# A planned three-stage kernel: new prices for VectorE's turns and GpSimd's copies, and one causal row block turned by way of DRAM

## The chip, the core and the metric

The kernel runs as one program on one core of a Trainium2 chip. The metric is the device time of one execution in microseconds (us); less is better. The core has five engines with a queue of instructions each: TensorE (PE; its weight loads are PEld), VectorE (DVE), ScalarE (ACT), GpSimd (POOL) and SyncE (SP), which here only issues DMAs. An engine takes its queue in order: an instruction that waits holds up all behind it.

## The reference

Three stages follow each other. All tensors are float32, except where a factor in the setup makes one float64 (the kernel decodes those on the chip).

```python
# 1. attention, masked by hash buckets: B, H, S, D = 2, 8, 768, 64; proj is 64 x 6
q_bits = (einsum('bhsd,dk->bhsk', q, proj) > 0); k_bits = the same of k
mask = bucket(q_bits)[:, :, :, None] == bucket(k_bits)[:, :, None, :]
scores = where(mask, q @ k^T / 8, -1e9);  attn = softmax(scores);  x = attn @ v       # as B, S, 512
# 2. four causal attention experts (512 -> 64), the best two of each token, weighted
for e in range(4):
    qe, ke, ve = x @ wq[e], x @ wk[e], x @ wv[e]
    a = softmax(where(causal, -1e9, qe @ ke^T / 8));  ye = a @ ve @ wo[e]
    out += gate[e] * ye
# 3. mixing of tokens and of channels on x = out: 2 x 768 x 512
theta = x @ w_theta;  zr, zi = x * cos(theta), x * sin(theta)
u = x + einsum('ts,bsd->btd', w_tok_r, zr) + einsum('ts,bsd->btd', w_tok_i, zi)
result = u + relu(u @ w_ch)
```

## The kernel before

**The work.** Stage 1 goes over 8 pairs of heads (2 batches of 4 pairs), stage 2 over the two expert pairs of both batches, stage 3 over blocks of 128 tokens. In stages 1 and 2 the unit of work is a `Unit`, a block of 128 query rows against up to 768 keys. For each: `scores` (TensorE, into a PSUM tile `ps`), `low` (VectorE: scale and row maximum, from `ps` to the tile `T`, L1007), `exp` (ScalarE, in place in `T`, L1015), `flip` (the turn of the row block, so that keys lie on partitions) and, for a whole group of units, `mix` (TensorE: the product with the values, L1060 in stage 1, L1082 in stage 2), and `gather` (ScalarE and GpSimd bring the product into `ob`).

**Two ways to turn.** In stage 1 eleven of a head pair's twelve row blocks are turned by VectorE in 32x32 pieces (L1022, 88 in all); their `mix` is 96 small matmuls on 32 rows (L1060), 192 records in the trace. All other blocks, and all of stage 2's, are turned by TensorE: one transpose for 128 columns into PSUM (L1026) and a copy back to `T` by ScalarE (L1035). Stage 3 has a third way in use already, for blocks of `u`: VectorE turns 32x32 pieces (`uw`, L1686), a DMA writes them to DRAM (`u_d`, L1688), and four DMAs bring them back with the pieces in their places (`uv`, L1690), before ScalarE reads them (L1698).

**Copies between partitions.** `shift` (L742) moves half a tile to other partitions by the engine that a letter names: A is ScalarE, P is GpSimd (`hi_pool`, L739), D is a DMA on SP's queue. `MOVESU` gives the letters of the four moves of `unstash`, which fetches an expert's operands back from DRAM (tile `op`) in stage 2.

**What sets the order.** The order of each engine's queue is not the order of the code. `Plan` reads the finished program, and `price` gives each instruction a step (when the engine is free for the next) and a latency, in ns. `forward` places the instructions one after the other, on the engine that can start first, with ranks from `backward`; `NUDGES` are random shifts of the ranks in a stretch of time; `fix` then writes the order into the program. The prices are used at build time alone. The lists `LP`, `PREP`, `LATE`, `FUSE`, `FM` and the like say beside which unit a job is written, which sets the order of tiles in the pools. `SPARE` is the number of extra matmuls on zeros (L867) in the first waits of TensorE. In `forward` the constants `FETCH` stand for TensorE's own instructions being fetched in parts of 256.

Of the kernel before, what the change touches and what calls it, by code (L numbers as in the profile page):

```python
# [38 lines left out]
LP = [0, 4.5, 5.5, 2.5, 8.5, 6, 9, 13, 10, 15.0, 17.5, 15]  # L39
PREP = [13.5, 9, 7.0, 9, 7.5]  # L40
# [6 lines left out]
LATE = [0, 2, 1, 1, 1, 1, 3, 4, 4, 4]  # L47
# [12 lines left out]
FUSE = 62  # L60
FS = 5
FM = 5
# [17 lines left out]
STAY = [[1, 4], [0, 5]]  # L80
MERGE = [11, 12]
MOVEG = 'P'
MOVESB = 'PD'
MOVESU = 'AADP'
# [3 lines left out]
LINE2 = [[[(0, 4)], [(0, 5)]], [[(1, 4)], [(1, 5)]], [[(0, 2), (1, 2)], [(0, 3), (1, 3)]],  # L88
# [6 lines left out]
SPARE = 35  # L95
# [100 lines left out]
def price(o):  # L196
# [20 lines left out]
    if o.eng == "DVE":  # L217
        if "Transpose" in o.kind and n > 32:
            return 215 + n * 1.045, 250 + n * 1.045
        crosses = o.r and o.r[0][2][0] // 32 != o.w[0][2][0] // 32  # L220
        if n < 30:
            s = 240 if o.kind == "InstReciprocal" else 170
        elif o.kind == "InstTensorScalarPtr" and src == ["S"]:
            s = 66 + n / 1.92
        else:
            s = 75 + n * 1.036
        if crosses:
            s = max(s, 80 + n * 1.18)
        if len(o.w) > 1:
            return 82 + n * 1.045, 202 + n * 1.045  # L230
        elif len(o.r) > 2 and o.kind == "InstTensorScalarPtr":
            s = 270 + n * 1.05
        return s, s + 80
# [10 lines left out]
    s = 140 + n * 2.17 if o.kind == "InstTensorTensor" else 165 + n * 0.82  # L244
# [463 lines left out]
def fused(ctx: ExitStack, tc: tile.TileContext, qT, kT, vP, vN, projd, wqk_d, wvg, wo, woT, wth, wtok, wch, out, waits, turns, runs,  # L708
          orders, desk, families, sequence):
    nc = tc.nc  # L710
# [95 lines left out]
    v_d = dram.tile([128, NT * E * D], F32, name="v_d")  # L806
    u_d = dram.tile([B * NT, 128, DM], F32, name="u_d")
# [16 lines left out]
    def ps_tile():  # L824
        return ps.tile([128, 1024], F32, name="ps", tag="ps", bufs=3)
# [125 lines left out]
    class Unit:  # L951


        def __init__(self, grp, rows, rs, last=False):
            self.grp, self.rs = grp, rs
            self.parts, off = [], 0
            for side, i in rows:
                w = (i + 1) * 128 if grp.causal else S
                self.parts.append((side, i, off, w))
                off += w  # L960
            self.w = off
            grp.done |= {(side, i) for side, i in rows}
            self.band = not grp.causal and rows[0][1] < NT - rs.old
            if not grp.causal:
                self.ends = rows[0][0] if last else None
                return
            ends = [c for c in range(NT // 2) if c not in grp.ended
                    and {(s, 2 * c + a) for s in (0, 1) for a in (0, 1)} <= grp.done]
            self.ends = ends[0] if ends else None
            grp.ended |= set(ends)  # L970
# [22 lines left out]
        def low(self):  # L993
# [3 lines left out]
            if not self.grp.causal:  # L997
                rs.n = self.parts[0][1] * NT
            self.P = rs.T[:, rs.n:rs.n + nb, :]
            for side, i, off, w in self.parts:  # L1000
                self.grp.at[side, i] = rs.T, rs.n + off // 128
# [18 lines left out]
        def flip(self):  # L1020
            if self.band:
                nc.vector.transpose(self.ss, self.ss)  # L1022
                return
            self.pt = ps_tile()
# [3 lines left out]
        def copy(self):  # L1028
            if self.band:
                return  # L1030
# [6 lines left out]
        def mix(self):  # L1037
# [36 lines left out]
            for j in range(n1):  # L1074
                for side in (0, 1):
                    (PT, a0), (_, a1) = g.at[side, 2 * c], g.at[side, 2 * c + 1]
                    half = slice(side * 64, side * 64 + 64)
                    if j < n0:
# [768 lines left out]
```

## Time and profile before

| | us |
|---|---|
| three runs, median (lowest, highest) | 496.0 (494.62, 496.75) |
| the profiled execution | 493.23 |
| its span, first to last instruction | 491.4 |
| TensorE busy | 465.1 (95%) |
| VectorE busy | 386.3 (79%) |
| ScalarE busy | 329.6 (67%) |
| GpSimd busy | 288.5 (59%) |

The profiled execution took 1.8 us more than its span, and 0.56% less than the median of the three runs. In its trace stage 1 of the first batch lies at about 9 to 125 us, stage 2's projections of the first batch and stage 1 of the second at 115 to 230, stage 2's units at 205 to 327, stage 3 from 305 to the end. A row of the views by instruction has start, duration, engine, line, operation, out<-in, and in brackets how long the engine was idle before and what ended that. "issue" as releaser means that the profile shows nothing that was waited for.

### The profile page before, as it was taken

To read this page: it belongs to the slowest core of one execution; us is meant where nothing else is said; L and a number is where in the kernel's file an instruction comes from. 1 tells how busy PE (TensorE), PEld (TensorE's weight loads), DVE (VectorE), ACT (ScalarE), POOL (GpSimd) and SP (SyncE) were. 2 spreads that over 40 slices of the span, in tenths; PEclk is the share of its full clock that TensorE was granted. 3 is DMA by queue.
4 is the path that set the end of the run, shared out by engine and by line. 5 is a ranking of instruction groups with operands and counts; after the bars stand their busy time and mean duration, and the time that the engine had idled before them with its cause. 6 is when DMAs were issued, how large, how long until landed. Compare 5 with 4: busy or idle time off the path is not lost.

```text
span 491.4 us, 13377 instructions
## 1 busy us (share of the span) xinstructions
PE 465.1 (95%) x5360; PEld 374.0 (76%) x5360; DVE 386.3 (79%) x668; ACT 329.6 (67%) x658; POOL 288.5 (59%) x243
## 2 busy tenths in 40 slices
PE   8889988989999999898999999999999999999997
PEld 3576866677898777676789877778888888878886
DVE  6999999688894999896677684849869999676543
ACT  7788867586454978869767689997667666571110
POOL 6997999888248479226920046058557697874000
PEclk9999999899999999999999999999999999999999
DMA  7544535445785545873448324512443445470542
GB/s 245 175 140 135 162 120 157 116 149 166 195 301 174 173 151 155 232 254 108 134 150 238 99 75 134 187 38 55 145 144 131 148 151 151 109 209 34 168 145 85
DMA packets 44249, 74.17 MB, mean 151 GB/s; under 512 B 6948, under 2 KB 13892, under 8 KB 44188
## 3 DMA queue, kind: packets, MB, share of 16 engines
q1 hardware_dynamic: 42028, 69.80, 46.4%
q10 hardware_dynamic: 2160, 3.52, 1.9%
q8 instruction: 42, 0.69, 0.6%
q14 instruction: 19, 0.16, 0.1%
HBM read 54.52 MB, written 15.91 MB: 143 GB/s over the span
## 4 chain that ended last, share of the span: by engine, by line
PE 72%; DVE 10%; ACT 7%; issue 4%; POOL 3%; DMA 2%; DVEq 0%; POOLq 0%; ACTq 0%
PE ps L1671 19%; PE ps L986 9%; PE ps L1060 9%; PE ps L1381 6%; PE wk L1585 5%; DVE T L1007 5%; PE wk L1600 4%; PE O L1060 4%; PE ps L1318 4%; PE ps L1026 4%; PE O L1082 3%; PE ps L1600 3%; ACT T L1015 3%; DVE T L1022 3%; PE ps L1068 1%
## 5 line engine op out<-in xcount | busy, mean ns | idle before, releaser
L1015 ACT ACTIVATE T<-T,m 128x768 f32<-128x768 f32 (+3 forms) x144 | 121.2, 844 | 31.8 <-DVE T L1007 31.2
L1007 DVE TENSOR_SCALAR_CACHE_REDUCE T<-ps 128x768 f32<-128x768 f32 (+3 forms) x144 | 115.5, 834 | 32.2 <-PE ps L991 15.0
L1022 DVE STREAM_TRANSPOSE T<-T 128x768 f32<-128x768 f32 x88 | 82.5, 960 | 5.5 <-ACT T L1015 5.1
L1671 PE MATMUL ps<-zh,tok 128*128 128x512 f32 x240 | 76.7, 390 | 0.0
L1060 PE MATMUL ps<-T,V 32*64 32x160 f32 (+1 forms) x1536 | 63.9, 312 | 8.4 <-DVE T L1007 3.3
L1060 PE MATMUL O<-T,V 32*64 32x160 f32 (+1 forms) x1536 | 65.0, 312 | 4.8 <-issue 4.7
L1060 PEld LDWEIGHTS ps<-T,V 32*64 32x64 f32 x1536 | 54.7, 131 | 13.9 <-issue 5.2
L986 PE MATMUL ps<-op 128*128 128x512 f32 (+5 forms) x256 | 60.1, 343 | 1.1 <-DVE op L1211 0.9
L1060 PEld LDWEIGHTS O<-T,V 32*64 32x64 f32 x1536 | 50.1, 131 | 6.4 <-issue 6.3
L1671 PEld LDWEIGHTS ps<-zh,tok 128*128 128x128 f32 x240 | 45.1, 188 | 9.7
L1671 PE MATMUL ps<-zl,tok 128*128 128x512 f32 x120 | 46.3, 391 | 0.0
L802 POOL TENSOR_TENSOR tok<-raw,tok 128x512 fp32r<-128x512 f32 x27 | 41.6, 1550 | 7.9 <-PE ps L1671 4.3
L986 PEld LDWEIGHTS ps<-op 128*128 128x128 f32 (+1 forms) x256 | 39.3, 191 | 8.4 <-issue 2.7
L1035 ACT COPY T<-ps 128x768 f32<-128x768 f32 (+2 forms) x36 | 28.6, 798 | 9.0 <-PE ps L1026 8.5
L739 POOL TENSOR_SCALAR op<-op 64x768 fp32r<-64x768 f32 x8 | 6.8, 853 | 45.6 <-ACT op L1397 28.7
L1026 PE MATMUL ps<-ident,T 128*128 128x128 f32 x216 | 30.7, 277 | 1.8 <-ACT T L1015 1.1
L1107 POOL TENSOR_TENSOR ob<-ob,W 64x768 f32<-64x768 f32 x16 | 29.4, 1835 | 1.3
L1026 PEld LDWEIGHTS ps<-ident,T 128*128 128x128 f32 x216 | 23.7, 141 | 5.8 <-ACT T L1015 2.5
L1015 ACT ACTIVATION_READ_ACCUMULATOR T<-T,m 128x1 f32 x144 | 27.2, 189 | 0.0
L1671 PEld LDWEIGHTS ps<-zl,tok 128*128 128x128 f32 x120 | 22.5, 188 | 4.9
L986 PE MATMUL ps<-op,sql 128*128 128x512 f32 x84 | 24.2, 366 | 2.1 <-DVE T L1007 1.1
L1620 POOL TENSOR_TENSOR kk<-kk,x 128x512 f32<-128x512 f32 x12 | 17.8, 1482 | 13.3 <-ACT kk L1619 13.3
(236 smaller groups left out, 1161.6 us busy)
## 6 DMA issues: line engine op xcount, KB each, us to landing
V<-in_vP_dram SPq DMA_DIRECT2D x48, 256.0 KB
raw<-in_wtok_dram SPq DMA_DIRECT2D x36, 256.0 KB
raw<-tok_d SPq DMA_DIRECT2D x27, 256.0 KB
tok_d<-g SPq DMA_DIRECT2D x18, 256.0 KB
rT<-r_d SPq DMA_DIRECT2D x22, 192.0 KB
qk_d<-op SPq DMA_DIRECT2D x8, 384.0 KB
op<-qk_d SPq DMA_DIRECT2D x8, 384.0 KB
out_dram<-o ACTq DMA_DIRECT2D x11, 256.0 KB
```

The source lines that it names most:

```text
L802: nc.gpsimd.tensor_sub(l, raw, f(h))
L986: one = nc.tensor.matmul(self.sp[:, c0:c1], lhs, rhs[:, c0 - off:c1 - off], start=a == 0, stop=last)
L1007: i = nc.vector.tensor_scalar(self.ss[:, off:off + w], self.sp[:, off:off + w], -0.125, NEG, op0=OP.mult, op1=OP.min, accum_out=m)
L1015: e = nc.scalar.activation(self.ss[:, off:off + w], self.ss[:, off:off + w], AF.Exp, bias=m, scale=-1.0, accum_out=self.grp.den[:, side, i ...
L1022: nc.vector.transpose(self.ss, self.ss)
L1026: nc.tensor.transpose(self.pt[:, j * 128:(j + 1) * 128], self.P[:, j, :], ident)
L1035: nc.scalar.copy(self.P, src)
L1060: together(nc.tensor.matmul(o[a][half * 64:half * 64 + 64, 0:nb * 32], V[band, n // 4, (n - a) % 4], T[band, 0:nb, n * 32:n * 32 + 32], st ...
L1107: nc.gpsimd.tensor_add(g.ob[keep], g.ob[keep], W[keep])
L1381: nc.tensor.matmul(pp[:, c0:c1], lhs[:, kd, e, :], rhs[kd][:, c0:c1], start=n == 0, stop=n == 3 * NK - 1)
L1600: nc.tensor.matmul(o, lhs[:, sl], rhs[:, kd, cols], start=n == 0, stop=n == 3 * NK - 1)
L1671: nc.tensor.matmul(yp[t], lhs[:, a, t, :], rhs[:, a], start=i == 0 and a == 0 and n == 0, stop=i == NT - 1 and a == 1 and n == 2)
```

## The change

Four things change in the code.

1. **Prices.** A turn by VectorE goes from 215 + 1.045 n ns to 95 + 1.045 n (n columns), its three-operand form from 270 + 1.05 n to 110 + 1.05 n; a copy by GpSimd from 165 + 0.82 n to 165 + 0.96 n, its two-operand form above 600 columns from 2.17 n to 2.28 n. With them the lists of places and all `NUDGES` are new (48 before, 78 now), so that the queues' orders differ nearly everywhere.
2. **One row block goes by DRAM.** Row block 5 (768 keys) of the first head of the second batch's first expert pair is turned like a block of `u`: one turn by VectorE into a tile `far`, one DMA to `far_d`, four back into `T`. Its six transposes on TensorE and its copy on ScalarE go. Its `mix` reads the block with other strides, so that the two row blocks that shared a matmul of 256 columns get one of 128 each: 67 instead of 72 with 256, 34 instead of 24 with 128.
3. **The last of `unstash`'s four moves** goes from GpSimd to a DMA (4 of them).
4. In stage 2 row block 5 comes ahead of row block 4, in places of `T` that are fixed for both; one extra matmul on zeros more.

```diff
-LP = [0, 4.5, 5.5, 2.5, 8.5, 6, 9, 13, 10, 15.0, 17.5, 15]
-PREP = [13.5, 9, 7.0, 9, 7.5]
+LP = [2, 4.5, 5.5, 2.5, 8.5, 6, 9, 13, 10, 15.0, 17.5, 15]
+PREP = [13.5, 9, 5.0, 9, 7.5]
-LATE = [0, 2, 1, 1, 1, 1, 3, 4, 4, 4]
+LATE = [0, 2, 1, 2, 1, 1, 3, 4, 4, 4]
-FUSE = 62
+FUSE = 60
-FM = 5
+FM = 3
+FAR = [4]
-MOVESU = 'AADP'
+MOVESU = 'AADD'
-LINE2 = [[[(0, 4)], [(0, 5)]], [[(1, 4)], [(1, 5)]], [[(0, 2), (1, 2)], [(0, 3), (1, 3)]],
+LINE2 = [[[(0, 5)], [(0, 4)]], [[(1, 4)], [(1, 5)]], [[(0, 2), (1, 2)], [(0, 3), (1, 3)]],
-SPARE = 35
+SPARE = 36
-    (288489, 5.7, 61.8, -1706), (998291, 190.5, 209.2, -4780), (727432, 453.6, 518.1, -1623), (283489, 92.7, 185.6, -838),
+    (403328, 264.5, 297.2, 538), (801660, 280.3, 290.3, 3416), (839062, 460, 492.5, -4580), (434552, 329.2, 405.9, -2079),
...
         if "Transpose" in o.kind and n > 32:
-            return 215 + n * 1.045, 250 + n * 1.045
+            return 95 + n * 1.045, 230 + n * 1.045
...
         elif len(o.r) > 2 and o.kind == "InstTensorScalarPtr":
-            s = 270 + n * 1.05
+            s = 110 + n * 1.05
...
-    s = 140 + n * 2.17 if o.kind == "InstTensorTensor" else 165 + n * 0.82
+    s = 140 + n * (2.28 if n > 600 else 2.17) if o.kind == "InstTensorTensor" else 165 + n * 0.96
...
+            self.far = grp.causal and rows[0][1] == 5 and 2 * grp.number - 8 + rows[0][0] in FAR
...
+            elif self.parts[0][1] > 3:
+                rs.n = self.parts[0][0] * 11 + (self.parts[0][1] - 4) * 5
...
+            if self.far:
+                w = pool.tile([128, S], F32, name="far", tag="far", bufs=1)[:, :self.w]
+                nb = self.w // 128
+                nc.vector.transpose(w.rearrange("p (b j x) -> p b j x", b=4, x=32),
+                                    self.ss.rearrange("p (j b x) -> p b j x", b=4, x=32))
+                d = far_d[next(fars)][:, :self.w]
+                nc.sync.dma_start(d, w)
+                for m in range(4):
+                    nc.sync.dma_start(self.ss[32 * m:32 * m + 32].rearrange("i (n y) -> i n y", n=4),
+                                      d.rearrange("(n i) (m y) -> m i n y", n=4, m=4)[m])
+                return
...
+                    one = g.at[side, 2 * c + 1][0]
+                    if isinstance(one, Unit):
+                        if j < n0:
+                            together(nc.tensor.matmul(self.O[half, 0], g.V[:, j, side, :], PT[:, a0 + j, :], start=j == 0,
+                                                      stop=False), j == side == 0, self.rs)
+                        rhs = one.ss.rearrange("p (n j x) -> p j n x", n=4, x=32)[:, j]
+                        together(nc.tensor.matmul(self.O[half, 1], g.V[:, j, side, :], rhs, start=False, stop=j == n1 - 1),
+                                 False, self.rs)
+                        continue
```

**SP's queue, the third head pair** (about 73 to 86 us of the trace before). `wraw`: expert weights, `V`: values, `raw<-in_kT`: keys, `r_d` and `rT`: softmax factors, out to DRAM and back. Before:

```order
L910 DMA r_d<-rows 4x32x32
L847 DMA wraw<-in_wqk_dram 128x512
L1151 DMA V<-in_vP_dram 128x512
L1134 DMA raw<-in_kT_dram 128x768
L1151 DMA V<-in_vP_dram 128x512 x2
L913 DMA rT<-r_d 64x768 x2
L847 DMA wraw<-in_wvg_dram 128x260
```

And now, the same place:

```order
L857 DMA wraw<-in_wvg_dram 128x260
L1184 DMA V<-in_vP_dram 128x512 x3
L1167 DMA raw<-in_kT_dram 128x768
L920 DMA r_d<-rows 4x32x32
L1184 DMA V<-in_vP_dram 128x512
L923 DMA rT<-r_d 64x768 x2
L1184 DMA V<-in_vP_dram 128x512 x2
```

The big weights `in_wqk` have left this group, and `r_d`, which waits for VectorE, now stands in the middle of it, ahead of `rT`.

**TensorE, between the fifth and the sixth `mix` of stage 1** (L1060 before, L1084 now; in the trace before the sixth starts at 80.11 us). Before, 20 score matmuls stand there, of which these are the last ones:

```order
L986 MATMUL ps<-skl,sqh 128x512
L986 MATMUL ps<-skl,sqh 128x256
L986 MATMUL ps<-skh,op 128x512
L986 MATMUL ps<-skh,op 128x256
L986 MATMUL ps<-skl,sqh 128x512
L986 MATMUL ps<-skl,sqh 128x256
L1060 MATMUL ps<-T,V 64x160 x4
L1060 MATMUL O<-T,V 64x160 x4
```

Now there are 24 and six transposes; this is the middle:

```order
L997 MATMUL ps<-skh,op 128x512
L997 MATMUL ps<-skh,op 128x256
L997 MATMUL ps<-skl,sqh 128x512
L997 MATMUL ps<-skl,sqh 128x256
L1050 MATMUL ps<-ident,T 128x128 x6
L997 MATMUL ps<-skh,op 128x512
```

Four score matmuls and a turn by TensorE have come between the two.

**VectorE and TensorE at the row block that goes by DRAM** (second batch's first expert pair). Before, on VectorE, the `low` of the pair's blocks (L1007) follow each other, with no turn among them:

```order
L1007 TENSOR_SCALAR T,m<-ps 128x768
L1398 TENSOR_TENSOR op<-ps,op 64x768
L1399 TENSOR_TENSOR op<-ps,op 64x768
L1568 TENSOR_TENSOR yl<-y,yh 128x768
L1007 TENSOR_SCALAR T,m<-ps 128x640
```

Now (`low` is L1020, the turn L1040):

```order
L1020 TENSOR_SCALAR T,m<-ps 128x768
L1040 STREAM_TRANSPOSE far<-T 128x768
L1020 TENSOR_SCALAR T,m<-ps 128x640
L1431 TENSOR_TENSOR op<-ps,op 64x768
L1432 TENSOR_TENSOR op<-ps,op 64x768
```

The turn stands right behind the `low` of its own block, and so waits on VectorE's queue for that block's `exp`. On TensorE that pair's first `mix` before, and behind it the start of the same now:

```order
L1026 MATMUL ps<-ident,T 128x128 x6
L1082 MATMUL O<-T,V 64x256 x10
L1082 MATMUL O<-T,V 64x128 x2
```

```order
L1050 MATMUL ps<-ident,T 128x128 x6
L1105 MATMUL O<-T,V 64x128
L1108 MATMUL O<-T,V 64x128
L1115 MATMUL O<-T,V 64x256
L1105 MATMUL O<-T,V 64x128
L1108 MATMUL O<-T,V 64x128
L1115 MATMUL O<-T,V 64x256
```

L1108 is the matmul that reads the block from DRAM; it is the second of the group, where a late block stops TensorE.

## Rows read from the trace of the kernel before

**Rows 1.** The page: span, busy time of the engines, instruction queue's packets

```profile
span 491.4 us, 13377 instructions
...
PE 465.1 (95%) x5360; PEld 374.0 (76%) x5360; DVE 386.3 (79%) x668; ACT 329.6 (67%) x658; POOL 288.5 (59%) x243
...
q8 instruction: 42, 0.69, 0.6%
```

**Rows 2.** Stages: length, busy us of each engine, PEclk, DMA share, GB/s

```profile
14.00:60.00 46.00, 41.51 (x838) 31.82 (x844) 44.10 (x79) 38.53 (x76) 40.84 (x40) 1.00 0.49 154
60.00:120.00 60.00, 52.79 (x1082) 40.97 (x1067) 52.24 (x96) 42.78 (x91) 52.87 (x47) 0.97 0.45 137
120.00:180.00 60.00, 58.43 (x1040) 50.80 (x1038) 50.59 (x97) 35.47 (x71) 31.25 (x29) 1.00 0.66 211
180.00:240.00 60.00, 53.85 (x1024) 42.26 (x1016) 48.22 (x96) 47.64 (x103) 37.06 (x33) 1.00 0.60 183
240.00:491.40 251.40, 246.87 (x1364) 202.22 (x1362) 181.49 (x281) 155.39 (x300) 116.79 (x81) 1.00 0.41 127
```

**Rows 3.** Waits of TensorE: us in total, times, longest

```profile
PE O L1060 <- issue: 4.7, 4, 2.4
...
PE ps L1060 <- issue: 2.4, 3, 1.3
```

**Rows 4.** TensorE in time, inside the sixth mix

```profile
82.22 0.29 PE L1060 MATMUL O<-T,V 32*64 32x160 f32 x1
84.94 0.36 PE L1060 MATMUL O<-T,V 32*64 32x160 f32 x3 [2.43 <-issue]
```

**Rows 5.** VectorE in time, the same stretch

```profile
82.11 1.83 DVE L1022 STREAM_TRANSPOSE T<-T 128x768 f32<-128x768 f32 x2
83.87 0.92 DVE L1007 TENSOR_SCALAR_CACHE_REDUCE T<-ps 128x768 f32<-128x768 f32 x1
...
89.83 0.96 DVE L1007 TENSOR_SCALAR_CACHE_REDUCE T<-ps 128x768 f32<-128x768 f32 x1 [4.13 <-PE ps L986]
```

**Rows 6.** Short stretches around it, columns as in rows 2

```profile
78.00:80.00 2.00, 2.00 (x12) 1.52 (x11) 2.00 (x6) 1.98 (x3) 1.84 (x3) 1.00 1.02 367
...
86.00:88.00 2.00, 2.00 (x36) 1.56 (x24) 0.00 (x0) 0.49 (x2) 1.84 (x2) 0.50 0.73 189
```

**Rows 7.** SP's queue in time ahead of it, first and last

```profile
74.49 0.41 SPq L847 DMA_DIRECT2D wraw<-in_wqk_dram  x1
...
78.13 1.14 SPq L913 DMA_DIRECT2D rT<-r_d  x2
```

**Rows 8.** TensorE in time: a unit's scores, transposes and a mix of stage 2

```profile
300.69 0.95 PE L986 MATMUL ps<-op 128*128 128x512 f32 x4
...
301.55 0.82 PE L1026 MATMUL ps<-ident,T 128*128 128x128 f32 x6
302.13 0.48 PE L986 MATMUL ps<-op 128*128 128x512 f32 x1
302.54 1.74 PE L1082 MATMUL O<-T,V 128*64 128x256 f32 x16
304.21 0.77 PE L1026 MATMUL ps<-ident,T 128*128 128x128 f32 x5
```

**Rows 9.** GpSimd and TensorE in time: a move of unstash, the first causal scores

```profile
205.20 0.83 POOL L739 TENSOR_SCALAR op<-op 64x768 fp32r<-64x768 f32 x1 [6.12 <-DMA op<-op]
...
219.29 0.88 PE L986 MATMUL ps<-op 128*128 128x512 f32 x4
```

**Rows 10.** VectorE in time: two turns of stage 3's blocks

```profile
393.72 0.70 DVE L1686 STREAM_TRANSPOSE uw<-x 128x512 f32<-128x512 f32 x1
...
452.76 0.71 DVE L1686 STREAM_TRANSPOSE uw<-x 128x512 f32<-128x512 f32 x1
```

**Rows 11.** ScalarE in time: the first readers of the two after DRAM

```profile
402.59 0.62 ACT L1698 CAST uTh<-uv 128x512 fp32r<-128x512 f32 x1
...
458.97 0.62 ACT L1698 CAST uTh<-uv 128x512 fp32r<-128x512 f32 x1 [11.57 <-DMA uv<-u_d]
```

More of the change, by code (lines that the diff above doesn't have):

```diff
@@ L806, in fused @@
     v_d = dram.tile([128, NT * E * D], F32, name="v_d")
+    far_d = dram.tile([8, 128, S], F32, name="far_d")
+    fars = itertools.count()
     u_d = dram.tile([B * NT, 128, DM], F32, name="u_d")
@@ L998, in low @@
                 rs.n = self.parts[0][1] * NT
+            elif self.parts[0][1] > 3:
+                rs.n = self.parts[0][0] * 11 + (self.parts[0][1] - 4) * 5
             self.P = rs.T[:, rs.n:rs.n + nb, :]
             for side, i, off, w in self.parts:
-                self.grp.at[side, i] = rs.T, rs.n + off // 128
+                self.grp.at[side, i] = (rs.T, rs.n + off // 128) if not self.far else (self, 0)
             rs.n += nb
@@ L1028, in copy @@
         def copy(self):
-            if self.band:
+            if self.band or self.far:
                 return
```

29 rows, old and new, of the table NUDGES are left out of this document.

## The prediction, as it was made before the run

> **What bounds the kernel now.** I read the page first, for which engine is full on average, and then the same busy times by stage, since an average over three stages says little. TensorE is busy 95% of the span [rows 1], but not evenly. From 240 us to the end it is busy 246.87 of 251.40 us [rows 2]: there the sum of its matmuls is the time, and an order can give back little. What can be won lies ahead of that. From 14 to 60 us VectorE is busy 44.10 of 46 us and is the bound itself. From 60 to 120 VectorE has 52.24 of 60 and TensorE 52.79, so neither is full and each waits for the other by turns. From 120 to 180, with the first batch's projections, TensorE has 58.43 of 60. From 180 to 240 it has 53.85 and VectorE 48.22. TensorE's idle time between 14 and 240 us is 4.49 + 7.21 + 1.57 + 6.15 = 19.4 us; that is all that a better order could win.
>
> Then the waits of TensorE. The largest kind inside the mixes of stage 1 has no releaser: "issue", 4.7 + 2.4 = 7.1 us in seven places [rows 3]. What that is can be read from the page: 42 packets of 0.69 MB, 16 KB each, on the instruction queue, for 2 x 5360 records of TensorE, which makes 255 records to a packet [rows 1]. TensorE's own code comes in parts by DMA; a mix (192 matmuls with as many weight loads) uses one and a half in some 4 us. The worst place shows what a late part costs. In the sixth mix TensorE stops at 82.2 us and starts again at 84.94, 2.43 us idle [rows 4]; VectorE, which had work for 3.5 us more, then lacks scores for 4.13 us [rows 5]; and the granted clock stands at 0.50 from 86 to 88 us [rows 6], which is the lower level, 1.2 GHz, right behind that pause. Just ahead of it the DMA engines are full, share 1.02 at 367 GB/s [rows 6]: SP had issued seven transfers from 74.49 to 78.13 us [rows 7].
>
> **The change part by part.** The sum is made against the profiled execution, 493.23 us (span 491.4 and 1.8 around it).
>
> *A, the row block by DRAM, on TensorE.* Six transposes take 0.58 us, from 301.55 to 302.13 [rows 8], and go: -0.58. The mix has ten matmuls of 128 columns more and five of 256 fewer: the same columns, but five matmuls, ten records, more. In a mix 16 records take 1.67 us, 0.104 each [rows 8]. If columns alone count, the split costs nothing; if every record costs the same, 1.04 us. I take the middle, +0.5, as the mixed row has both widths. A: -0.1, between -0.6 and +0.5. VectorE's additional turn (0.88 us, from 82.11 to 83.87 for two [rows 5]) falls into a stretch where VectorE has 181.49 of 251.40 us [rows 2], and ScalarE loses a copy: nothing.
>
> *B, does the block come back in time?* Its mix waits for it on TensorE, and all later matmuls stand behind. For the cover I count TensorE's new queue between the block's scores and that mix: 28 transposes (2.7 us at 0.097), 12 matmuls of other mixes (24 records, 2.5 us) and 63 others with 19,072 columns. A unit's scores with their mask are 1664 columns in 0.86 us, 300.69 to 301.55 [rows 8], so these take 9.9 us. Cover: 15.1 us. The way is bounded by stage 3's blocks, which go it already: from the turn's start to the first reader 402.59 - 393.72 = 8.9 us, and 458.97 - 452.76 = 6.2 us at the quickest [rows 10, 11]. The new block is half as long again: 6.2 to 13.3 us. Its `low` (0.92 us [rows 5]) and `exp`, taken as long, come ahead: 8 to 15.2 us. Value: 0; end of the range +0.5. Behind the turn on VectorE stands the `low` of the next block, whose scores come some 20 matmuls later, so the turn's wait for `exp` holds nobody up. On SP the read-backs wait for the write, and behind them stand a move and weights of stage 3 that start to be used some 10 us later.
>
> *C, late code.* The order changes both sides of the stall in the sixth mix. Between the fifth and the sixth mix there are now 24 score matmuls and six transposes instead of 20 score matmuls, so the code has longer to come. And SP's group there is lighter: before, 256 + 256 + 384 + 512 + 384 = 1792 KB in one go by the shapes in its queue; now 130 + 768 + 384 = 1282 KB, then `r_d`, which waits for VectorE. At 367 GB/s [rows 6] that is 4.9 against 3.5 us of full DMA engines. 1.4 us less of a crowd and at least 0.58 us (the transposes) more time is 2.0 us, most of the 2.43 us that the part came late. At most the chain wins VectorE's 4.13 us; at least nothing, if the crowd only meets another part. The other late parts (4.7 us) I leave as they are: 16 mixes with 192 records are still there. C: -2.4, the wait itself, between -4.1 and 0.
>
> The Trainium skill says in "Runtime: NRT & Kernel Launch", section "Instruction fetch mechanics", that the sequencer streams 16 KiB blocks of 256 instructions by a DMA queue of its own and that crossing a block is "mostly hidden". The parts of 16 KB agree with rows 1; the hiding does not with rows 4. By that rule C would be 0 and the sum -1.6.
>
> *D, the new prices.* A turn's price falls from 1018 to 898 ns at 768 columns; two in a row take 1.76 us [rows 5], 0.88 each. So before, the planner gave VectorE 88 x 0.12 = 10.6 us of work that it does not have, all in stage 1, and set TensorE's and ScalarE's work beside it accordingly. No row shows what a plan with the right price wins. From 14 to 60 us VectorE is full and from 120 to 180 us TensorE: nothing there. In the other two stretches TensorE's idle time without the 7.1 us of late code is 7.21 + 6.15 - 7.1 = 6.3 us. All of it is the lower end, -6.3; a new order that trades one wait for another can also lose, by about as much as one half of it, +3. I take a quarter of it, -1.5, nearer to nothing, since the old order too was sorted by the same search and no single wait of it is removed by name. GpSimd's dearer copies move work off a queue that is 59% busy [rows 1]: nothing.
>
> *E, unstash's last move by DMA.* Four copies of 0.83 us leave GpSimd. The earliest in the old order ran at 205.20 us, having itself waited 6.12 us for a DMA, and the first causal scores started at 219.29 [rows 9]: 13 us of cover for a transfer. Cost 0; without that cover it would be one transfer of up to 6 us, once. The extra spare matmul stands in a wait.
>
> Sum: -0.1 + 0 - 2.4 - 1.5 + 0 = -4.0, so 489.2 for the profiled execution, 0.81% less. The runs' median, 496.0, is 0.56% above that execution; 0.81% off it is 492.0 us.
>
> **The rivals.** *No change.* The crowd on the DMA engines only meets another part of the code, and the waits are reshuffled to the same total. For it: stage 1 has VectorE at 96% and then TensorE at 97% in two of its four stretches [rows 2]. Against it: the worst stall has its own cause, and SP's group has changed just there. Then A alone is left: 495.9 us.
>
> *A second late part.* The 7.1 us come from seven of sixteen mixes, so a part that is late is common; the new order of SP puts 1282 KB in one group, and other groups elsewhere. If the sixth mix's stall stays and one other mix gets one of that kind, VectorE lacks scores for another 4.13 us [rows 5]: 496.0 - 0.1 + 4.1 = 500.0 us, slower. It decides from the point where the DMA engines are at share 1.0 for over 2 us while a mix runs. Against it: two of the sixteen mixes had nothing but 20 score matmuls between them and the mix before, the sixth among them, and in the new order none has so little.
>
> *The block comes late.* With all of the way at its upper end and another 3 us in SP's queue, the mix waits some 3 us, and C and D are eaten up but for 1 us: 495.0 us, within no change.
>
> *The block comes far too late.* If the strided read back from DRAM took 38 us instead of about a third of the quickest way's 6.2 us, then with some 6 us for `low`, `exp`, turn and write it would end 29 us past the cover, and the time would be 496.0 - 4.0 + 29 = 521 us. Rows 10 and 11 speak against it: the same kind of read, in runs of 512 bytes, is over in 6.2 to 8.9 us with all that is ahead of it. Hence one chance in a hundred. The 38 us are an estimate from the Trainium skill, which warns in "VectorE: DVE Perf Modes", section "The three transpose paths", that a plain DMA copy with access-pattern strides for the transpose is 19 times slower than the transposing one (19 x 2 us).
>
> **How the numbers follow.** Forecast, C and D together: 0.58. No change by either of the two ways: 0.28. A second late part: 0.13. Far too late: 0.01. The forecast's own range is 488 to 493.5. For 8 in 10 the lower end has C at its best and D at three times its value (-0.1 - 4.1 - 4.5 = -8.7 us, cut to 487.0, since both at once are rare); the upper end, 498.2, takes in no change with the spread of the runs and leaves the slower cases out. About 0.5%, 2.5 us, is what a measurement of this kernel can tell from no change (the three runs span 0.43%): faster 0.58, same 0.28, slower 0.14.
>
> **What would show it.** Right: in the changed trace the sixth mix shows less than 1 us of "issue", no stretch at a clock of 0.50 behind it, and VectorE no wait of 4 us near 86 us; the row block's mix starts with no wait for a DMA; from that pair's end to the end the time is unchanged within 1 us, so that the gain lies ahead of 240 us. Wrong: total "issue" in the mixes as large as 7 us again (C), TensorE's idle time from 60 to 240 us as large as before without it (D), a wait for `T<-far_d` (B), a mix of that pair longer by over 1 us (A), or scores that wait for `op<-op` (E).

## The result, and the profile after

| | median, us | lowest to highest | runs |
|---|---|---|---|
| before | 493.89 | 488.94 to 500.53 | 20 |
| changed | 496.38 | 494.25 to 500.04 | 20 |

The changed kernel takes 1.0077 of the time before (95% interval 1.0049 to 1.0105; disturbed executions are left out of it, so it is not the quotient of the medians): it is slower by 0.8%, where the forecast had it faster by 0.8%. Its profiled execution took 497.67 us, 4.4 more than that of before.

The page of the changed kernel, as [rows 1]: span, busy time, instruction queue.

```profile
span 495.9 us, 13388 instructions
...
PE 467.9 (94%) x5365; PEld 377.4 (76%) x5365; DVE 390.7 (79%) x669; ACT 329.4 (66%) x657; POOL 284.1 (57%) x239
...
q8 instruction: 42, 0.69, 0.6%
```

TensorE's work is nearly the same (5365 records for 5360). Of the 4.5 us that the span grew it is busy for 2.8 more and idle for 1.7 more. The stages, as [rows 2], the last one to the new end:

```profile
14.00:60.00 46.00, 40.87 (x732) 32.13 (x732) 40.42 (x72) 34.50 (x68) 38.02 (x36) 0.93 0.48 152
60.00:120.00 60.00, 52.90 (x1154) 40.96 (x1153) 53.65 (x97) 45.37 (x95) 52.69 (x48) 0.97 0.43 130
120.00:180.00 60.00, 58.50 (x861) 49.63 (x860) 51.87 (x94) 34.09 (x68) 33.77 (x31) 1.00 0.67 214
180.00:240.00 60.00, 52.36 (x1162) 41.41 (x1162) 49.91 (x92) 46.31 (x95) 34.70 (x31) 1.00 0.63 180
240.00:495.90 255.90, 252.02 (x1418) 207.31 (x1417) 184.57 (x296) 159.21 (x316) 115.56 (x80) 1.00 0.43 133
```

Up to 60 us all three computing engines did less than before, VectorE 40.42 us for 44.10, ScalarE 34.50 for 38.53. Fixed windows cut the two programs at different work, so the next step goes by a mark that both have, the start of the sixteenth mix of stage 1. TensorE in time there, before and then changed (start, us, engine, line, names, count):

```profile
226.00 0.36 PE L1060 MATMUL ps<-T,V 32*64 32x160 f32 x4
```

```profile
231.47 0.36 PE L1084 MATMUL ps<-T,V 32*64 32x160 f32 x4
```

All of the loss, 5.5 us, lies ahead of it; from there to the end the changed kernel takes 264.4 us and the one before 265.4. The waits of TensorE (in total, times, longest), as [rows 3], changed:

```profile
PE ps L1084 <- DVE T L1020: 7.2, 10, 0.8
PE O L1084 <- issue: 2.8, 2, 1.4
PE ps L1084 <- issue: 2.6, 4, 1.0
PE ps L997 <- DVE bits L1284: 2.5, 3, 1.3
PE ps L997 <- ACT T L1059: 2.2, 4, 0.8
```

and the first of these lines in the kernel before:

```profile
PE ps L1060 <- DVE T L1007: 3.3, 4, 1.1
```

Late code ("issue") fell, from 7.1 to 5.4 us. That these waits are for code shows in the packets of the instruction queue: all 13 of them inside the mixes, in both kernels, end 2.2 to 2.7 us after such a packet has started. What rose is the wait of a mix for VectorE's `low`: ten mixes wait at their head now, four did before. Read off the starts of the first matmul of each mix, the seven times between the end of one mix and the start of the next, from the first mix to the eighth, are (us):

| kernel | | | | | | | | sum |
|---|---|---|---|---|---|---|---|---|
| before | 7.45 | 9.03 | 3.80 | 10.45 | 3.81 | 9.70 | 5.25 | 49.5 |
| changed | 8.49 | 7.84 | 7.61 | 7.64 | 6.48 | 7.80 | 6.97 | 52.8 |

Long and short gaps in turn have become even ones, and their sum is 3.3 us larger. The eight gaps after them grew from 83.8 to 86.8 us, the stretch ahead of the first mix shrank from 24.1 to 22.3, and the sixteen mixes went from 72.2 to 73.3. The mixes should have shrunk with the late code, but three of them ran in part at the lower clock, where before it was one [rows 6]. The changed kernel's short stretches in the second, third and seventh mix, and behind the late code of the sixth (columns as in [rows 2], the last four PEclk, DMA share, GB/s at the end):

```profile
36.00:39.00 3.00, 2.95 (x88) 2.96 (x96) 2.74 (x6) 2.93 (x7) 2.83 (x4) 0.50 0.03 8
50.00:52.00 2.00, 2.00 (x62) 2.00 (x54) 2.00 (x5) 1.48 (x3) 2.00 (x2) 0.50 0.17 36
98.00:100.00 2.00, 2.00 (x64) 1.69 (x56) 2.00 (x4) 1.03 (x2) 2.00 (x2) 0.50 0.13 27
...
86.00:90.00 4.00, 2.58 (x95) 1.90 (x78) 3.19 (x5) 2.65 (x7) 3.69 (x4) 1.00 0.65 170
```

Those three mixes took 4.90, 5.77 and 5.74 us, the same ones before 4.02, 4.63 and 5.17. How much of this there is differs between executions: the granted clock of the changed kernel's twenty is between 0.986 and 1.000 of full speed, and the profiled one, with 0.990, is among the lower. The ten at 0.996 and above still took 494.25 to 496.78 us, so the loss does not hang on it.

### The profile page after: what moved, and what is told of

Its sections match the earlier page's. It is cut to its first block, busy times and chain, and to the rows that moved or that the text cites. A ratio compares the mean times of both kernels' runs of the same rounds, so it can differ in the third digit from the quotient of the medians.

```text
span 495.9 us, 13388 instructions
## 1 busy us (share of the span) xinstructions
PE 467.9 (94%) x5365; PEld 377.4 (76%) x5365; DVE 390.7 (79%) x669; ACT 329.4 (66%) x657; POOL 284.1 (57%) x239
## 3 DMA queue, kind: packets, MB, share of 16 engines
q1 hardware_dynamic: 43068, 71.37, 47.5%
## 4 chain that ended last, share of the span: by engine, by line
PE 71%; DVE 16%; ACT 7%; issue 3%; DMA 2%; SPq 0%; DVEq 0%
PE ps L1704 20%; PE ps L1084 9%; PE ps L997 8%; DVE T L1020 8%; PE ps L1414 7%; PE wk L1618 6%; DVE T L1035 5%; PE wk L1633 4%; ACT T L1028 4%; PE O L1084 3%; PE ps L1050 3%; PE ps L1633 3%; PE O L1115 3%; PE ps L1351 2%; ACT T L1059 1%
## 5 line engine op out<-in xcount | busy, mean ns | idle before, releaser
L1028 ACT ACTIVATE T<-T,m 128x768 f32<-128x768 f32 (+2 forms) x144 | 121.2, 843 | 41.6 <-DVE T L1020 40.1
L1020 DVE TENSOR_SCALAR_CACHE_REDUCE T<-ps 128x768 f32<-128x768 f32 (+2 forms) x144 | 115.9, 833 | 25.9 <-PE ps L997 14.6
L1084 PE MATMUL ps<-T,V 32*64 32x160 f32 (+1 forms) x1536 | 67.8, 326 | 9.8 <-DVE T L1020 7.2
L1084 PEld LDWEIGHTS ps<-T,V 32*64 32x64 f32 x1536 | 58.2, 139 | 17.3 <-DVE T L1020 11.1
L1084 PE MATMUL O<-T,V 32*64 32x160 f32 (+1 forms) x1536 | 67.6, 326 | 2.8 <-issue 2.8
L997 PE MATMUL ps<-op 128*128 128x512 f32 (+5 forms) x256 | 62.2, 346 | 1.9 <-DVE op L1244 1.5
L1084 PEld LDWEIGHTS O<-T,V 32*64 32x64 f32 x1536 | 52.4, 138 | 2.6 <-issue 2.6
L747 POOL TENSOR_SCALAR ob<-W 64x768 f32<-64x768 f32 x16 | 13.3, 828 | 27.7 <-ACT W L1131 21.7
L997 PE MATMUL ps<-skh,op 128*128 128x512 f32 (+1 forms) x84 | 25.0, 375 | 3.9 <-ACT T L1059 2.2
L785 DVE SCALAR_TENSOR_TENSOR g<-raw,g 128x512 uint32<-128x512 uint32 x26 | 27.8, 1069 | 0.6
L1050 PEld LDWEIGHTS ps<-ident,T 128*128 128x128 f32 x210 | 24.1, 140 | 3.8 <-ACT T L1028 0.9
```

The lines of the kernel that those rows point to most:

```text
L997: one = nc.tensor.matmul(self.sp[:, c0:c1], lhs, rhs[:, c0 - off:c1 - off], start=a == 0, stop=last)
L1020: i = nc.vector.tensor_scalar(self.ss[:, off:off + w], self.sp[:, off:off + w], -0.125, NEG, op0=OP.mult, op1=OP.min, accum_out=m)
L1028: e = nc.scalar.activation(self.ss[:, off:off + w], self.ss[:, off:off + w], AF.Exp, bias=m, scale=-1.0, accum_out=self.grp.den[:, side, i ...
L1050: nc.tensor.transpose(self.pt[:, j * 128:(j + 1) * 128], self.P[:, j, :], ident)
L1084: together(nc.tensor.matmul(o[a][half * 64:half * 64 + 64, 0:nb * 32], V[band, n // 4, (n - a) % 4], T[band, 0:nb, n * 32:n * 32 + 32], st ...
```

## The experiments

**1. The turn itself, orders kept.** Theory R: the order before was laid out for turns of 1018 ns that take 895, so it has VectorE early; the new one, laid out for what they take, has no reserve, and each delay goes through. Rivals: VectorE paces both alike (V); half clock and late code are the cause (C). Both plans were made as they are and then emitted with one thing changed, so that each engine's order is the same.

```diff
-                nc.vector.transpose(self.ss, self.ss)
+                nc.vector.transpose(*[self.ss if sequence is None else self.ss[:, :self.w - 128]] * 2)
```

> The kernel before, each engine's order kept; the 88 turns of stage 1 on VectorE handle 640 of 768 columns (the last 128 columns of every block are left unturned), so each is about 0.13 us shorter, 11.8 us of VectorE in all. Theory R (reserve): this order was laid out for turns of 1018 ns and real ones take 895, so it has VectorE early enough; shorter turns give 0 to 1.5 us. Rival V (VectorE paces stage 1 in both orders alike): 6 to 12 us faster, as much as in the new order. Rival C (half clock and late code, not VectorE): within 1 us, as in the new order.

Measured: 1.0011 (0.9978 to 1.0044), so nothing won, as theory R and rival C had it.

> The changed kernel, each engine's order kept, the same 88 turns 0.13 us shorter (the last 128 columns of every block left unturned). Theory R: the new order has no room between VectorE's last tile and the mix that waits for it (ten waits of 0.7 us each at the head of a mix), so it gains 3 to 6 us and ends at or below the kernel before: ratio 0.995 to 1.002. Rival V: 6 to 12 us, and the old order as much. Rival C: within 1 us of the changed kernel, ratio 1.006 to 1.010.

Measured: 1.0078 (1.0051 to 1.0105), the same as the changed kernel's 1.0077. Theory R had 0.995 to 1.002 and fails here; rival C had this result. The turns did get shorter, 0.83 us for 0.96. But where in the profiled executions the gaps lost 2.5 us and the stretch ahead of the first mix 0.5, the mixes took 2.5 more (75.7 us for 73.3), for in them TensorE waited longer for late code:

```profile
PE O L1084 <- issue: 5.4, 6, 1.6
PE ps L1084 <- DVE T L1020: 2.0, 4, 0.7
...
PE ps L1084 <- issue: 0.7, 1, 0.7
```

(its waits from 23 to 125 us). In the other direction, a small memset behind each turn:

```diff
-                nc.vector.transpose(self.ss, self.ss)
+                i = nc.vector.transpose(self.ss, self.ss)
+                if sequence is not None:
+                    desk.behind[i.ins.name] = nc.vector.memset(more, 0.0).ins
```

> The kernel before, orders kept, with one memset of 128x96 by VectorE behind each of the 88 turns of stage 1 (0.13 to 0.17 us each, 11 to 15 us of VectorE in all; nothing is left out). Theory R: about the room that this order has, so 1 to 5 us slower. Rival V: 8 to 13 us slower, like the new order. Rival C: within 1.5 us.

Measured: 1.0030 (1.0002 to 1.0057), 1.5 us.

> The changed kernel, orders kept, with the same memset behind each of the 88 turns. Theory R: nearly every memset lands in front of a waiting mix: 8 to 13 us slower than the changed kernel (ratio 1.024 to 1.034 against the kernel before). Rival V: 8 to 13 us, and the old order as much. Rival C: within 1.5 us of the changed kernel.

Measured: 1.0156 (1.0113 to 1.0198), 3.9 us over the changed kernel. The memset was cheaper than I had put it: it adds 0.10 us to the time from a turn's start to the start of what follows, so 8.8 us in all. The new order passes on nearly half of that, the old one a sixth, so the new one looks the tighter. But its six executions also had a lower granted clock, 0.986 on average for 0.994 in the changed kernel, and how much of the 3.9 us that is was not separated. V fails in all four, R in the two on the new order, and C in this last one alone. The loss is not simply that the real turn is too long for the new order, since a shorter one wins nothing: with it the waits for `low` at the mixes' heads fell from 4.8 to 2.0 us (23 to 125 us), and the late code rose by 4.2.

**2. Prices or settings?** The order follows from the prices and from the settings, and then the table of nudges shifts it. So both tables were emptied (`NUDGES = []`), and old and new settings were planned with old and new prices.

```diff
-            return 215 + n * 1.045, 250 + n * 1.045
+            return 95 + n * 1.045, 230 + n * 1.045
...
-            s = 270 + n * 1.05
+            s = 110 + n * 1.05
...
-    s = 140 + n * 2.17 if o.kind == "InstTensorTensor" else 165 + n * 0.82
+    s = 140 + n * (2.28 if n > 600 else 2.17) if o.kind == "InstTensorTensor" else 165 + n * 0.96
```

> The kernel before with its table of nudges empty, planned anew; the reference of a square of four: old or new settings (LP, PREP, LATE, LINE2, FUSE, FM, SPARE, MOVESU, far block) by old or new prices, all without nudges. Theory P (prices): a plan laid with prices equal to the pitches keeps no reserve, so in both rows the new prices are 2 to 6 us slower. Rival S (settings): the new settings are slower by 2 to 6 us at either price. Rival N (the table): no steady sign in rows or columns, so that the loss lies in the table of nudges and the one order it makes. This one: 492 to 497 us, ratio 1.000 to 1.012, by all.

Measured: 1.0143 (1.0059 to 1.0227), above what all three theories had.

> The same without nudges, the three price lines of the change put in. Theory P: 2 to 6 us over the one with old prices. Rival S: equal to it within 2 us. Rival N: anything within 5 us on either side.

Measured: 1.0300 (1.0244 to 1.0357).

> The changed kernel with its table of nudges empty. Theory P: 2 to 6 us over new settings with old prices. Rival S: 2 to 6 us over old settings with new prices. Rival N: near the changed kernel, and no steady sign.

Measured: 1.0248 (1.0173 to 1.0323).

> The changed kernel with its table empty and the three price lines as before. Theory P: the better of the two with new settings by 2 to 6 us. Rival S: 2 to 6 us over old settings with old prices. Rival N: no steady sign.

Measured: 1.0178 (1.0109 to 1.0246).

The new prices are slower in both rows, by 1.6% with the old settings and 0.7% with the new ones (the latter pair's intervals overlap). The new settings do no harm: 0.35% over the old ones with old prices, 0.5% under them with new prices, both within the intervals. S falls, P has the sign (its 2 to 6 us were 7.4 us in the first row and 2.8 in the second). Each plan was run only four times. And each kernel's own table of nudges is worth some 1.5% of its plan (1.0143 to 1, and 1.0248 to 1.0077).

**3. Which price?** From new settings with new prices, no nudges, one price at a time was put back.

> New settings, no nudges, GpSimd's and the three-operand prices new; the turn's price alone back at 1018 ns. Theory T (the turn's price sets the pattern): with 1018 the planner lays long and short gaps between the mixes in turn (8 to 10 us, 4.5 to 6 us), and PE waits at the head of every second mix; with 898 every gap is near 7.7 us and PE waits at nearly every head. So gaps 2 to 8 sum to 48 to 50 us (52.6 in the run with all prices new), and the kernel is 3 to 7 us faster than that one (503.8 against a kernel before of 491.4): 496.5 to 501. Rival G (GpSimd's price): even gaps as there, within 2 us of 503.8.

Measured: 1.0014 (0.9977 to 1.0050), against 1.0248 with that one line the other way.

> New settings, no nudges, the turn's price new at 898; GpSimd's prices alone back (copies 795). Theory T: even gaps of 7 to 8 us, 52 to 55 us in gaps 2 to 8, within 2.5 us of the run with all prices new (503.8). Rival G: 3 to 7 us faster than that one, with long and short gaps.

Measured: 1.0352 (1.0308 to 1.0396).

Theory T holds in sign and in pattern, and missed both sizes: the turn's price alone costs 2.3%, some 11.5 us where 3 to 7 were expected, and the other plan came 5 us over the one with all prices new, where 2.5 were allowed. GpSimd's new prices are a gain, 1.0% (1.0352 to 1.0248; the intervals just touch). With the turn's old price the new prices of GpSimd and of the three-operand form together gain 1.6% (1.0178 to 1.0014), clear of both intervals; the three-operand price was never put back alone. The gaps tell all eight plans apart by the turn's price:

| turn's price | kernel | seven gaps, us | ratio |
|---|---|---|---|
| 1018 | before | 49.5 | 1 |
| 1018 | old settings, old prices | 49.9 | 1.0143 |
| 1018 | new settings, old prices | 50.2 | 1.0178 |
| 1018 | turn's price back | 47.5 | 1.0014 |
| 898 | changed | 52.8 | 1.0077 |
| 898 | old settings, new prices | 54.2 | 1.0300 |
| 898 | new settings, new prices | 52.6 | 1.0248 |
| 898 | GpSimd's price back | 53.5 | 1.0352 |

So do the mixes that wait at their head for a `low`: 10 to 12 of the sixteen in the four plans with 898, 4 to 7 in the four with 1018. But neither orders the ratios: two plans with 1018, both without nudges, are slower than the changed kernel, which has them.

What an even gap costs is seen at the fourth mix of new settings with new prices. TensorE and then VectorE in time:

```profile
60.53 0.62 PE L977 MATMUL ps<-skh,op 128*128 128x512 f32 x2 [0.78 <-DVE T L1000]
60.98 0.51 PE L977 MATMUL ps<-skl,sqh 76*128 76x512 f32 x2
62.27 0.36 PE L1064 MATMUL ps<-T,V 32*64 32x160 f32 x4 [0.78 <-DVE T L1000]
```

```profile
58.64 0.97 DVE L1015 STREAM_TRANSPOSE T<-T 128x768 f32<-128x768 f32 x1
59.53 0.92 DVE L1000 TENSOR_SCALAR_CACHE_REDUCE T<-ps 128x768 f32<-128x768 f32 x1
60.38 0.97 DVE L1015 STREAM_TRANSPOSE T<-T 128x768 f32<-128x768 f32 x1
61.28 0.92 DVE L1000 TENSOR_SCALAR_CACHE_REDUCE T<-ps 128x768 f32<-128x768 f32 x1
```

VectorE does a turn, a `low`, a turn, a `low`, and TensorE waits for each `low`, because that is what frees one of the three `ps` tiles that scores and mix share. With the turn's price back the same mix comes without a wait, right behind its scores:

```profile
56.87 0.52 PE L977 MATMUL ps<-skl,sqh 76*128 76x512 f32 x2
57.31 0.36 PE L1064 MATMUL ps<-T,V 32*64 32x160 f32 x4
```

There VectorE did one `low` after another ahead of the turns, which it does beside the mix (VectorE in time):

```profile
56.28 0.95 DVE L1000 TENSOR_SCALAR_CACHE_REDUCE T<-ps 128x768 f32<-128x768 f32 x1
57.16 0.95 DVE L1000 TENSOR_SCALAR_CACHE_REDUCE T<-ps 128x768 f32<-128x768 f32 x1
58.03 0.08 DVE L1000 DVE_READ_ACCUMULATOR T<-ps 128x1 f32 x1
58.03 2.69 DVE L1015 STREAM_TRANSPOSE T<-T 128x768 f32<-128x768 f32 x3
```

The waits at the mixes' heads from 23 to 125 us, turn's price new and then back:

```profile
PE ps L1064 <- DVE T L1000: 5.7, 8, 0.8
```

```profile
PE ps L1064 <- DVE T L1000: 2.7, 3, 1.1
```

These waits are only a part of the 2.3%. The sixteenth mix starts 14.1 us later with the new price. TensorE in time, new and then back:

```profile
237.34 0.36 PE L1064 MATMUL ps<-T,V 32*64 32x160 f32 x4
```

```profile
223.24 0.36 PE L1064 MATMUL ps<-T,V 32*64 32x160 f32 x4
```

Of that the fifteen gaps are 7.5 us and the stretch ahead of the first mix -1.8; the other 8.4 us lie inside the fifteen mixes. There the late code is longer, over the whole trace with the new price and then with the old one back:

```profile
PE ps L1064 <- issue: 4.4, 4, 2.2
PE O L1064 <- issue: 3.7, 4, 1.7
```

```profile
PE O L1064 <- issue: 2.4, 3, 0.9
PE ps L1064 <- issue: 2.2, 2, 1.6
```

and the granted clock is lower: 0.985 on average over the four executions with the new price, 0.997 over the eleven with the old one.

**4. The far block.** With the turn's price back and no nudges, FAR emptied.

```diff
-FAR = [4]
+FAR = []
```

> The kernel with the turn's price back and no nudges, with FAR empty: all causal row blocks turned by TensorE. Without nudges the plan of stage 1 is the same, so the two differ in the causal stage alone. Theory T says nothing of it; term A of the forecast: within 0.6 us of the kernel with the far block (ratio 1.000 to 1.003 against the kernel before). Rival F (the far block and its four DMAs cost something, or collide with other transfers): 1 to 3 us faster without it.

Measured: 1.0073 (1.0044 to 1.0102), so if anything slower without the far block, against 1.0014. Most of that isn't its doing. Against what was expected, the two orders differ by a few rows in stage 1 too, and in the profiled runs the sixteenth mix starts at 223.2 with it and 226.2 us without, and from there to the end it is 267.4 and 267.9. Rival F fails; what the far block is worth in its own stage is too small to tell from one execution each. The run shows something else: an edit that has no part in stage 1 moved it by 3.0 us, through the order. So a difference of half a per cent between two plans can be chance; the 2.3%, with the pattern in all eight plans, hardly is.

**5. A version that beats both.** The settings and GpSimd's prices of the change, the turn's price of before, and a table of nudges made for that plan, twice.

```diff
-            return 95 + n * 1.045, 230 + n * 1.045
+            return 215 + n * 1.045, 250 + n * 1.045
...
 NUDGES = [
-    (403328, 264.5, 297.2, 538), (801660, 280.3, 290.3, 3416), (839062, 460, 492.5, -4580), (434552, 329.2, 405.9, -2079),
+    (855749, 59.6, 74.6, -4436), (941537, 210.3, 220.3, -1590), (477976, 368.1, 448.1, -3281), (490598, 163.3, 178.3, 1230),
...
```

> The kernel with the turn's price back at 1018 and a new table of 23 nudges, made for that plan (chosen by the planner's own end, reckoned with turns at 898 and at 998 ns and with VectorE's results up to 0.2 us late, so that the order keeps some reserve). Theory T: the tables won 1.4 to 1.7% of their own plan before, so 0.985 to 0.998 against the kernel before, faster than both. Rival L (the plan with the turn's price back was a lucky one, 1.0014 without any table): 0.998 to 1.010.

Measured: 0.9943 (0.9913 to 0.9973), 489.76 us beside 493.06.

> The same with another table, begun from the same first ten nudges and continued apart from it. Theory T: 0.985 to 0.998 too. Rival L: 0.998 to 1.010, or the two tables more than 1% apart.

Measured: 0.9933 (0.9902 to 0.9963), 490.00 us.

Two orders agree, and rival L fails in both. They are not independent: both tables were begun from the same ten nudges and made for the same plan. Against the changed kernel they are 1.3 and 1.4% faster by the quotient of the ratios. That is not the turn's price alone, since their tables were chosen with some reserve in the planner's reckoning, and none was made in that way for a plan with 898. The first one's seven gaps sum to 47.3 us, and its sixteenth mix starts at 222.3. They won 0.7 to 0.8% of their plan, half of what the older tables did.

## Why the prediction was wrong, step by step

*D is the step that failed*, in sign and in size. It said that the turns' old price gave VectorE "10.6 us of work that it does not have" and that a plan with the right price wins some of TensorE's idle time, -1.5 us, with +3 as the upper bound. The trace has +5.5 us ahead of the sixteenth mix, although the late code fell by 1.7, and experiment 3 shows the turn's price alone to be worth +2.3% of the time without nudges. By the prediction's own sign, too, D is wrong: TensorE's idle time from 60 to 240 us without late code went from 7.8 to 10.8 us (14.9 - 7.1 and 16.2 - 5.4). A price in a planner is not time that somebody spends. It decides what stands ahead of what. In the fourth mix of experiment 3 it shows as follows, and the gaps and the waits at the heads have the same pattern in all eight plans: at 1018 ns a turn was put behind the `low` that frees a `ps` tile, and the mixes came in pairs, one after a short gap without a wait; at 898 the turn is put ahead of it, each gap is even, and TensorE waits for VectorE at ten mixes instead of four. Three more errors are in that step. The bound of +3 was one half of the idle time that could be won, and nothing limits a loss to that. The stretch from 14 to 60 us was set to zero, as VectorE was full in it [rows 2]; but a full engine is only a reason against a gain, and its 44.10 us fell to 40.42. And GpSimd's prices were costed at nothing, where they win 1.0% (and 1.6% together with the three-operand price).

What remains open is why the planner, which reckons with the real duration, prefers the slower order, and why the mixes themselves lose more than half of what the turn's price costs in experiment 3, with late code and the lower clock. That these two hit the even order harder is a guess. Experiment 1 only half supports it: a memset costs that order 3.9 us for 1.5, some of it perhaps by the clock, but a shorter turn gives it nothing. How much of the changed kernel's own 0.8% is the turn's price was not measured either: its nudges belong to its plan, and a table is worth about 1.5%.

*C* was right in direction, with 1.0 us for 2.4. In the sixth mix the wait for code fell from 2.43 to 1.42 us, so the sign that was named, less than 1 us, did not come:

```profile
87.71 0.34 PE L1084 MATMUL O<-T,V 32*64 32x160 f32 x1 [1.42 <-issue]
```

The other two signs came: there is no stretch at 0.50 behind it, and VectorE's longest wait from 84 to 96 us is 1.8 us, for 4.13 [rows 5]. All late code fell by 1.7 us. It did not reach the end: the second, third and seventh mix lost 2.6 us together in the profiled execution, with the clock at 0.50 in each. Nor is it shown that the spacing, "24 score matmuls and six transposes instead of 20", gave the code its time. The gap ahead of the sixth mix is 6.48 us in the changed kernel and 3.81 before; with the turn's price back it is 4.9 us, in the old order with the memsets 4.3, and in neither is there any late code in that mix.

*A* was forecast at -0.1, with +0.5 for the split of the matmuls. The far block's mix before, and the last row of the same mix now:

```profile
296.60 2.60 PE L1082 MATMUL O<-T,V 128*64 128x256 f32 x24
```

```profile
303.67 0.27 PE L1115 MATMUL O<-T,V 128*64 128x128 f32 x1
```

As it now starts at 301.28, it takes 2.66 us for 2.60: the split costs 0.06 us, which is the bound of "columns alone", and A is about -0.5. *B* was right for TensorE: the far block's mix starts straight behind other work, with no wait for a DMA (TensorE in time):

```profile
300.47 0.88 PE L1050 MATMUL ps<-ident,T 128*128 128x128 f32 x6
301.28 0.32 PE L1105 MATMUL O<-T,V 128*64 128x128 f32 x1
```

as its turn was at 287.6 us, 13.7 us before. GpSimd has one wait of 2.4 us that the trace puts down to the block's DMAs, for weights of stage 3; no wait of TensorE shows in it. *E* was right: none of TensorE's waits is for a move by DMA. From the end of the far block's mix to the end the time changed by 0.3 us (192.2 to 191.9), within the 1 us that was allowed.

*The rivals.* The second late part had the sign, 500.0 us for 496.4, but not the mechanism: no second part of the code came 2.4 us late. No change was nearer in kind, since its waits are reshuffled; it lacked that they can add up to a loss of 0.8%. A late block, by little or by far, is out with B: its read-backs were issued from 291.1 to 292.9 us, and the mix at 301.28 waits for none. The base had moved too: the three runs before the prediction had 496.0 us, the twenty have 493.89.

## What to carry to other kernels

A duration that a planner uses is a knob of the order, and correcting it to the measured one can cost more than any instruction it describes: change one price at a time, and measure each with the searched corrections (here the nudges) off. When an edit reorders, compare the two orders at the places where the engines meet (here: does the step that frees the shared buffer stand ahead of the mix or behind a longer one) before any duration. And a stretch in which an engine is full can still become longer.

## What the runs showed of the hardware

In the changed order, taking 0.13 us from each of 88 instructions of VectorE gave nothing on TensorE: the gaps became shorter, and the mixes waited for their code instead, 6.1 us from 23 to 125 us for 1.9 in the changed kernel. And a VectorE operation whose operands all lie in SBUF took 2.20 us beside a GpSimd one, where it takes 0.69 alone; VectorE and GpSimd in the changed kernel:

```profile
123.41 2.20 DVE L784 SCALAR_TENSOR_TENSOR g<-raw,g 128x512 uint32<-128x512 uint32 x1
125.64 0.69 DVE L785 SCALAR_TENSOR_TENSOR g<-raw,g 128x512 uint32<-128x512 uint32 x1
```

```profile
123.18 1.88 POOL L948 TENSOR_TENSOR xl<-x,xh 128x768 fp32r<-128x768 f32 x1
```

It is not so each time. Of the 52 such operations in the changed kernel's trace, the 27 with no GpSimd instruction beside them took 0.64 to 0.70 us; of the 25 with one, 16 took 1.17 to 2.20 and nine 0.68 to 0.69. What decides between the two is not shown.
